# Pooled keys and values in half tiles, their accumulating loads two steps apart, and reciprocals at the end of a step

## The chip, the cores and the metric

The kernel runs on one core of a Trainium2 chip. The metric is the device time of one execution in microseconds (us); lower is better. Three runs of the kernel before gave a median of 1055.34 us (1048.17 to 1058.86). The profile shows one more execution, of 1054.12 us.

## The reference

Attention over keys and values that are averaged in groups of eight, and then a feed-forward layer with a squared relu:

```python
# B, H, S, D = 8, 8, 576, 64; Sp = 72; x: 4608 x 512; w_in: 512 x 2048; w_out: 2048 x 512
k_p = k.reshape(B, H, Sp, 8, D).mean(axis=3)
v_p = v.reshape(B, H, Sp, 8, D).mean(axis=3)
scores = (1 / sqrt(D)) * q @ k_p^T
attn = exp(scores - max(scores)); attn = attn / (sum(attn) + 1e-9)
x = (attn @ v_p), heads side by side
h = maximum(x @ w_in, 0)
out = (h * h) @ w_out
```

## The kernel before, in words

The 4608 tokens are worked through in nine chunks of 512. A chunk has 16 steps, one for each 128 of the 2048 hidden columns (`steps`, L618). In a step PE computes hidden columns (`hidden`, L564, tiles `h`) and then adds the hidden columns of three steps earlier to the outputs (`project`, L596, tiles `o`). From chunk 2 on the hidden product goes by pairs of steps in seven block products (`seven`, L524) on sums and differences of blocks of the input, the operands B11, T1, T2 and so on (`x_operand`, L497, tiles `x_B` and `x_T`). Operands are split in a high and a low part (`split`, L110; `gh` and `gl` for the hidden values), and three products of the parts are added. `w_o`, the weights of the second layer, is kept in DRAM in split form, and each step's 512 KB are fetched over SP's queue, by the program one step before they are used (`fetch_weights`, L208).

Beside it the attention of the next chunk runs, pair of heads by pair of heads, in stages that a table puts on steps (`STEADY`, L83): turning q (`transpose_q`), scores on PE (`sps`), the maximum over keys on POOL (`mx`), exponents, their sum on POOL (`tot`), the sum's way over DRAM into 128 partitions (`rs`, `rc`), the reciprocal on DVE (`reciprocals`, L390, tile `rr`), its way back (`rd`, `rb`), and the product with the values (`weigh_values`, L463, `av`). Within chunk positions 0 to 15, `mx` stands at steps 2, 6, 10, 14, `tot` at 0, 4, 8, 12, the reciprocals at 3, 7, 11, 15.

A batch's pooled keys and values are needed once for each batch. Batches 0 and 1 are loaded at the start; batches 2 to 7 are loaded while other chunks run (`kv_steps`, L724). Eight rows are to be added into one. `load_sums` (L251) does this by four transfers for each kind: the first, on SP's queue, writes two rows of each group side by side; the other three, on POOL's queue, add theirs onto it, each as two transfers of four heads, 144 KB. `pool` (L263) then adds the two on DVE (tiles `kq` and `vp`), and `turn_k` (L273) turns the keys on PE (`kps`). All go through one tile with the tag `two` and one buffer, so the values' first load waits until the keys have been added. By `KV0` and `KV_AT` (L84, L86) the keys' transfers stand at steps 1 to 4 of the chunk two before the one that first needs the batch, their addition at 6 and the turning at 7; the values' transfers at 7 to 10 and their addition at 12.

Every engine works in program order, which the loop at L754 writes out step by step. In a step it emits, in this order: PE's hidden product and attention products; the fetch of `w_o`; the split of hidden values; `project`; the rest of the seven products' sums on DVE; the evacuations of what PE made; the loads (q, `load_sums`); then the other stages in the order of the table, among them `pool` and `reciprocals` (L783); then the relu and square on ACT (`activate`), and last the differences and operands of the next chunk (L795). All plain transfers are issued from SP's queue in that order too, and a transfer that waits holds those behind it. Instructions go through a recording helper, so the profile names L34 for nearly all of them; groups are told apart by tiles.

Of the kernel before, what the change touches and what calls it, by code (L numbers as in the profile page):

```python
# [9 lines left out]
F32 = mybir.dt.float32  # L10
# [4 lines left out]
ALU = mybir.AluOpType  # L15
# [22 lines left out]
def pooled_attn_relu2_ffn(  # L38
# [16 lines left out]
    PE, DVE, ACT, GP, SP = (InOrder(tc, e) for e in (nc.tensor, nc.vector, nc.scalar, nc.gpsimd, nc.sync))  # L55
    B, H, S, D = q.shape
# [4 lines left out]
    POOL = 8  # L61
    SP_ = S // POOL
    NPAIR = H // 2
    NFC = DFF // P
# [16 lines left out]


    STEADY = ((-23, -19, -15, -11), (0, 1, 3, 5, 6, 6, 7, 8))  # L83
    KV0 = -34  # L84
    EARLY = ((-15, -12, -10, -7), (0, 1, 2, 3, 4))
    KV_AT = (("k", 3), ("v", 9))  # L86
    X_AT = (("B11", -9), ("B22", -2), ("T1", -2), ("T3", -2), ("T2", -1), ("B21", -1), ("T4", -1))
    STIR = 10

# [2 lines left out]
    sb = ctx.enter_context(tc.tile_pool(name="sb", bufs=2))  # L92
# [9 lines left out]
    def load(dst, src):  # L102
        loads.append((dst, src))

    def issue_loads():
        for dst, src in loads:
            dma(dst, src)
        loads.clear()
# [67 lines left out]
    def catch_up():  # L176
        while behind:
            behind.pop(0)()
# [36 lines left out]
    def new_batch(b):  # L215
        if b not in kv:
            kv[b] = sb.tile([SP_, H, D], F32, name=f"vp_{b}", tag="vp", bufs=2)
# [28 lines left out]
        for i in range(2):  # L246
            DVE.tensor_reduce(kv[b][:, 2 * p + i, :], t[:, i].rearrange("p (o d) -> p d o", d=D), axis=AX.X, op=ALU.add)

    two = {}

    def load_sums(kind, b, j):  # L251

        if j == 0:
            new_batch(b)
            two[kind] = sb.tile([SP_, H, 2 * D], F32, name=f"{kind}2_{b}", tag="two", bufs=1)
        src = {"k": k, "v": v}[kind][b].rearrange("h (s j o) d -> j s h (o d)", j=POOL // 2, o=2)[j]
        if j == 0:
            load(two[kind], src)
        else:
            for n in range(0, H, H // 2):  # L260
                GP.dma_start(two[kind][:, n:n + H // 2], src[:, n:n + H // 2], accum_op=ALU.add)

    def pool(kind, b):  # L263
        t = two.pop(kind)
        if kind == "v":
            dst = kv[b]
        else:
            dst = sb.tile([SP_, H, D], F32, name=f"kq_{b}", tag="kq", bufs=1)
            for p in range(NPAIR):
                loaded["kp", b, p] = dst[:, 2 * p:2 * p + 2, :]  # L270
        DVE.tensor_tensor(dst, t[:, :, :D], t[:, :, D:], op=ALU.add)

    def turn_k(b, pairs=range(NPAIR)):  # L273

# [26 lines left out]
    def segments(c):  # L301
        t, segs = c * CH, []
        while t < (c + 1) * CH:
            b = t // S
            n = min((b + 1) * S, (c + 1) * CH) - t
            segs.append((b, t - c * CH, n))
            t += n
        return segs
# [255 lines left out]
    def hidden(c, fc):  # L564
        if c < PLAIN:
            hps = [(fc, plain(c, fc))]
        else:
            hps = seven(c, fc)
            if fc % 2 == 0:
                return hps  # L570

        def activate():
            for f, hp in hps:
                if c == 0:
                    r = gts[c, f] = sb.tile([P, CH], F32, name=f"r_{c}_{f}", tag="gl" if f % 2 else "gh", bufs=3)
                else:
                    r = gts[c, f] = sb.tile([P, CH], F32, name=f"r_{c}_{f}", tag="r", bufs=2)
                ACT.activation(r, hp, AF.Relu)
            for f, _ in hps:
                ACT.activation(gts[c, f], gts[c, f], AF.Square)  # L580

        return (activate, None, None) if c >= PLAIN else (None, None, activate)

    def split_hidden(c, fc):
        if c == 0:
            return
        gh = sb.tile([P, CH], F32R, name=f"gh_{c}_{fc}", tag="gh", bufs=3)
        gl = sb.tile([P, CH], F32R, name=f"gl_{c}_{fc}", tag="gl", bufs=3)
        r = gts[c, fc]
        gts[c, fc] = (gh, gl)  # L590
        ACT.copy(gh, r)
        behind.append(lambda: DVE.tensor_tensor(gl, r, gh.bitcast(F32), op=ALU.subtract))
# [3 lines left out]
    def project(c, fc):  # L596
        if fc == 0:
            accs[c] = [ps_o.tile([P, 512], F32, name=f"o_{c}_{t}", tag=f"o{t}") for t in range(NTT)]
        g, key = gts.pop((c, fc)), ("o", fc)
        for t in range(NTT):  # L600
            tt = slice(t * P, (t + 1) * P)
            if c == 0:
                prods = [(g[:, tt], wf[key].rearrange("p a n -> p (a n)"))]
            else:
                prods = [(g[x][:, tt], wt[key][:, w, :]) for x, w in three]
            for i, (a, w) in enumerate(prods):
                PE.matmul(accs[c][t], lhsT=a, rhs=w, start=fc == 0 and i == 0, stop=fc == NFC - 1 and i == len(prods) - 1)

        def store():
            for t in range(NTT):  # L610
                ob = half_tile("ob", f"ob_{c}_{t}")
                ACT.copy(ob, accs[c][t])
                dma(out[c * CH + t * P:c * CH + (t + 1) * P, :], ob)

        return store if fc == NFC - 1 else None
# [5 lines left out]
    def at(step, f, *a):  # L621
        work.setdefault(max(step, -PRO), []).append((f, a))
# [22 lines left out]
    t = ps_a.tile([P, 512], F32, name="stir", tag="a")  # L645
# [60 lines left out]
    t = 1e9  # L706
    for key in reversed(keys):
        t = min(t - 1 / RATE, need[key] - 1 - MARGIN)
# [15 lines left out]
    def kv_steps(b, s):  # L724
        for kind, start in KV_AT:
            for j in range(POOL // 2):
                at(s + start + j, load_sums, kind, b, j)
            at(s + start + POOL // 2 + 1, pool, kind, b)
        at(s + KV_AT[0][1] + POOL // 2 + 2, turn_k, b)

    ready = {0, 1}
    stages = (transpose_q, scores, exponents, send_sums, fetch_sums, reciprocals, fetch_reciprocals, weigh_values)
    for c in range(1, NCH):
        first, offsets = EARLY if c < PLAIN else STEADY
        names = (transpose_q, token_scores, token_normalise, token_turn, weigh_values) if c < PLAIN else stages
        for b, _, _ in segments(c):
            if b not in ready:
                ready.add(b)
                kv_steps(b, c * NFC + KV0)
        if c >= PLAIN:  # L740
            at(c * NFC - 3, x_sums, c)
            for name, d in X_AT:
                at(c * NFC + d, x_operand, c, name)
        for p in range(NPAIR):
            s = c * NFC + first[p]
            at(s - QL, load_q, c, p)
            for d, f in zip(offsets, names):
                at(s + d, f, c, p)


    last = (to_float32, split_quarter, sum_of_quarters, store_weights)
    on_pe = (turn_k, scores, token_scores, token_turn, weigh_values)
    store = None
    for s in range(-PRO, len(steps) + LAG):  # L754
        todo = work.get(s, [])
        soon, then, activate = hidden(*steps[s]) if 0 <= s < len(steps) else (None, None, None)
        later = [f(*a) for f, a in sorted(((f, a) for f, a in todo if f in on_pe), key=lambda x: x[0] is weigh_values)]
        for f, a in todo:
            if f is fetch_weights:
                f(*a)  # L760
        if 0 <= s - 2 < len(steps):
            split_hidden(*steps[s - 2])
        if store:
            store()
        store = project(*steps[s - LAG]) if s >= LAG else None
        if s % 2:
            catch_up()
        if soon:
            soon()
        for f in later:  # L770
            f()
        if then:
            then()
        catch_up()
        first = (load_q, load_sums)
        for f, a in todo:
            if f in (fetch_sums, fetch_reciprocals):
                f(*a)
        for f, a in todo:
            if f in first:  # L780
                f(*a)
        issue_loads()
        for f, a in todo:  # L783
            if f not in first + on_pe + last + (x_sums, x_operand, fetch_weights, fetch_sums, fetch_reciprocals):
                f(*a)
        keys = [a[0] for f, a in todo if f is to_float32]
        if keys:
            to_float32(*keys)
        for f, a in todo:
            if f in last[1:] and f is not sum_of_quarters:  # L790
                f(*a)
        issue_loads()
        if activate:
            activate()
        for kind in (x_sums, x_operand, sum_of_quarters):  # L795
            for f, a in todo:
                if f is kind:
                    f(*a)
# [31 lines left out]
```

## Time and profile before

| what | value |
|---|---|
| median of three runs | 1055.34 us |
| profiled execution, its own time | 1054.12 us |
| span of that execution | 1052.3 us |
| PE busy | 938.6 us, 89% of the span |
| DVE, ACT, POOL busy | 555.3, 509.4, 421.0 us |
| mean granted clock of TensorE | 0.932 |
| time of DMA engines on SP's queue, on POOL's queue | 39.9%, 8.8% of 16 engines' span |

A row of waits reads: engine and tile, what ended the wait, then us in total, times, and the longest. A row of the time line reads: start and duration in us, engine, operation, out<-in, shape, count, and in brackets the engine's idle time just before and what ended it. "issue" means that nothing the profile shows was waited for. A row of windows reads: from and to, length, for each engine busy us and count of instructions, then the mean granted clock (1.00 is full), the DMA engines' share, and GB/s. SPq is SP's queue.

### The profile page before, as it was taken

How to read it: one execution, taken by the hardware profiler on the slowest of the kernel's cores; microseconds unless marked ns; L12 is line 12 of the kernel's file. 1: busy time of each engine (PE TensorE's matmuls, PEld its weight loads, DVE VectorE, ACT ScalarE, POOL GpSimd, SP SyncE). 2: the span in 40 equal slices, each digit the busy share in tenths (PEclk: the TensorE clock that was granted, in tenths of full speed). 3: DMA queues.
4: the chain of work that ended last, by engine and by line, in shares of the span. 5: the costliest groups of instructions: out<-in, count | busy, mean ns of one | idle time of the engine just before them, and what ended most of it. 6: DMA issues, size and time to landing. Idle time of an engine off the chain costs nothing. (4 is left out here: it accounts for less than half of the span.)

```text
span 1052.3 us, 14125 instructions
## 1 busy us (share of the span) xinstructions
PE 938.6 (89%) x5050; PEld 740.4 (70%) x5050; DVE 555.3 (53%) x959; ACT 509.4 (48%) x1015; POOL 421.0 (40%) x234
## 2 busy tenths in 40 slices
PE   5799988995979897988799796979699999999998
PEld 3344443574758676877688685868588888889997
DVE  4884657733567675635274345534375465535231
ACT  2573645553356544644256344544265555535433
POOL 6731124425544455436344554445545333410000
PEclk6598989998989999998899898989899999999999
DMA  8894431484724464465536463546435344223801
GB/s 224 248 255 98 107 99 61 151 223 116 216 56 137 101 158 113 139 124 125 123 113 158 81 151 75 152 93 155 92 121 152 101 134 159 91 93 124 315 1 40
DMA packets 161480, 138.72 MB, mean 132 GB/s; under 512 B 98633, under 2 KB 126281, under 8 KB 161409
## 3 DMA queue, kind: packets, MB, share of 16 engines
q1 hardware_dynamic: 132608, 127.13, 39.9%
q0 software_dynamic: 28800, 10.68, 8.8%
q8 instruction: 40, 0.66, 0.2%
q14 instruction: 32, 0.25, 0.1%
HBM read 119.65 MB, written 18.06 MB: 131 GB/s over the span
## 5 line engine op out<-in xcount | busy, mean ns | idle before, releaser
L34 PE MATMUL o<-w_o,gh 128*128 128x512 f32 x1024 | 330.0, 404 | 8.2 <-DMA w_o<-kept 8.1
L34 POOL PARTITION_ALL_REDUCE tot<-sc x56 | 191.9, 3474 | 178.0 <-issue 153.4
L34 PEld LDWEIGHTS o<-w_o,gh 128*128 128x128 f32 x1024 | 189.6, 194 | 54.8 <-issue 13.3
L34 PE MATMUL o<-w_o,gl 128*128 128x512 f32 x512 | 203.4, 397 | 0.0
L34 PE MATMUL h<-x_T,w_S 128*128 128x256 f32 x1008 | 136.7, 290 | 3.3 <-DVE x_T L34 1.7
L34 ACT ACTIVATE r<-h 128x512 f32<-128x512 f32 x144 | 85.1, 594 | 110.9 <-PE h L34 57.2
L34 POOL PARTITION_ALL_REDUCE mx<-sc x56 | 108.4, 1982 | 64.4 <-ACT sc L34 63.2
L34 PEld LDWEIGHTS h<-x_T,w_S 128*128 128x128 f32 x1008 | 130.2, 199 | 5.3 <-DVE x_T L34 2.9
L34 PE MATMUL h<-x_B,w_A 128*128 128x256 f32 x672 | 101.7, 288 | 31.1 <-ACT r L34 31.1
L34 DVE TENSOR_TENSOR gl<-r,gh 128x512 fp32r<-128x512 f32 x128 | 108.1, 858 | 34.6 <-ACT gh L34 34.6
L34 PEld LDWEIGHTS h<-x_B,w_A 128*128 128x128 f32 x672 | 94.0, 196 | 37.2 <-ACT r L34 33.2
L34 PEld LDWEIGHTS o<-w_o,gl 128*128 128x128 f32 x512 | 98.6, 193 | 22.3
L34 ACT COPY u<-h 128x256 f32<-128x256 f32 x112 | 41.6, 371 | 134.0 <-DVE h L34 79.2
L34 DVE TENSOR_TENSOR h<-h,u 128x256 f32<-128x256 f32 x168 | 72.7, 433 | 51.2 <-ACT u L34 29.4
L34 POOL DMA_DIRECT2D k<-in_k_dram x36 | 43.7, 1214 | 125.2 <-issue 119.3
L34 POOL DMA_DIRECT2D v<-in_v_dram x36 | 44.2, 1227 | 120.1 <-issue 62.9
L34 ACT ACTIVATE sc<-sc 72x512 f32<-72x512 f32 x56 | 34.5, 631 | 117.8 <-DVE sc L34 117.8
L34 ACT ACTIVATE r<-r 128x512 f32<-128x512 f32 x144 | 84.2, 625 | 1.0
L34 ACT CAST gh<-r 128x512 fp32r<-128x512 f32 x128 | 78.6, 614 | 1.0 <-PE o L34 0.4
L34 DVE TENSOR_TENSOR u<-h,u 128x256 f32<-128x256 f32 x56 | 23.7, 423 | 80.5 <-ACT u L34 79.6
L34 PE MATMUL o<-wf_o,r 128*128 128x512 f32 x128 | 65.1, 656 | 0.0
L34 DVE TENSOR_TENSOR st<-qs,st 64x512 fp32r<-64x512 f32 x56 | 46.9, 837 | 25.1 <-ACT st L34 24.3
(89 smaller groups left out, 1204.1 us busy)
## 6 DMA issues: line engine op xcount, KB each, us to landing
w_o<-kept SPq DMA_DIRECT2D x128, 512.0 KB
out_dram<-ob SPq DMA_DIRECT2D x36, 256.0 KB
raw_i<-in_moe_w_in_dram SPq DMA_DIRECT2D x16, 512.0 KB
raw_o<-in_moe_w_out_dram SPq DMA_DIRECT2D x16, 512.0 KB
kept<-w_o SPq DMA_DIRECT2D x16, 512.0 KB
rb<-rd SPq DMA_DIRECT2D x56, 128.0 KB
k<-in_k_dram POOLq DMA_DIRECT2D x36, 144.0 KB, 4.1
v<-in_v_dram POOLq DMA_DIRECT2D x36, 144.0 KB, 5.4
```

What stands on the lines that cost most here:

```text
L34: return lambda *a, **k: self.tc.keep_in_program_order(f(*a, **k))
```

## The change

Three things change. The tile `two` becomes two tiles of four heads with two buffers, in the same space as before; the first load is split in two as well, and `pool` adds in two halves, each from its own tile. The accumulating transfers stand two steps apart: the keys' at steps 15 (of the chunk before), 1, 3 and 5, their addition at 7 and the turning at 8; the values' at 7, 9, 11 and 13, their addition at 15. And `reciprocals` leave the middle of the step for its end, behind the operands of the next chunk, with the transfer `rd` that they issue.

```diff
     STEADY = ((-23, -19, -15, -11), (0, 1, 3, 5, 6, 6, 7, 8))
-    KV0 = -34
     EARLY = ((-15, -12, -10, -7), (0, 1, 2, 3, 4))
-    KV_AT = (("k", 3), ("v", 9))
+    KV_AT = (("k", -33), ("v", -25))
...
-    two = {}
+    two, HALF = {}, H // 2
 
     def load_sums(kind, b, j):
 
         if j == 0:
             new_batch(b)
-            two[kind] = sb.tile([SP_, H, 2 * D], F32, name=f"{kind}2_{b}", tag="two", bufs=1)
         src = {"k": k, "v": v}[kind][b].rearrange("h (s j o) d -> j s h (o d)", j=POOL // 2, o=2)[j]
-        if j == 0:
-            load(two[kind], src)
-        else:
-            for n in range(0, H, H // 2):
-                GP.dma_start(two[kind][:, n:n + H // 2], src[:, n:n + H // 2], accum_op=ALU.add)
+        for n in range(2):
+            if j == 0:
+                two[kind, n] = sb.tile([SP_, HALF, 2 * D], F32, name=f"{kind}2_{b}_{n}", tag="two", bufs=2)
+                load(two[kind, n], src[:, n * HALF:(n + 1) * HALF])
+            else:
+                GP.dma_start(two[kind, n], src[:, n * HALF:(n + 1) * HALF], accum_op=ALU.add)
 
     def pool(kind, b):
-        t = two.pop(kind)
...
-        DVE.tensor_tensor(dst, t[:, :, :D], t[:, :, D:], op=ALU.add)
+        for n in range(2):
+            t = two.pop((kind, n))
+            DVE.tensor_tensor(dst[:, n * HALF:(n + 1) * HALF], t[:, :, :D], t[:, :, D:], op=ALU.add)
...
             for j in range(POOL // 2):
-                at(s + start + j, load_sums, kind, b, j)
-            at(s + start + POOL // 2 + 1, pool, kind, b)
-        at(s + KV_AT[0][1] + POOL // 2 + 2, turn_k, b)
+                at(s + start + 2 * j, load_sums, kind, b, j)
+            at(s + start + POOL, pool, kind, b)
+        at(s + KV_AT[0][1] + POOL + 1, turn_k, b)
...
-                kv_steps(b, c * NFC + KV0)
+                kv_steps(b, c * NFC)
...
-            if f not in first + on_pe + last + (x_sums, x_operand, fetch_weights, fetch_sums, fetch_reciprocals):
+            if f not in first + on_pe + last + (x_sums, x_operand, reciprocals, fetch_weights, fetch_sums, fetch_reciprocals):
                 f(*a)
...
-        for kind in (x_sums, x_operand, sum_of_quarters):
+        for kind in (x_sums, x_operand, reciprocals, sum_of_quarters):
```

POOL, the keys of batch 5, before (steps 2 to 6 of chunk 3; ISA rows are all-reduces, `mx` the maximum and `tot` the sum of a pair of heads, DMA rows the accumulating transfers):

```order
L34 ISA mx_2_0_3503<-sc_2_3502 72x512
L34 ISA mx_2_1_3504<-sc_2_3502 72x512
L34 DMA k_5_3434<-in_k_dram 72x4x128 x6
L34 ISA tot_2_0_3650<-sc_2_3502 72x512
L34 ISA tot_2_1_3651<-sc_2_3502 72x512
L34 ISA mx_3_0_3771<-sc_3_3770 72x512
L34 ISA mx_3_1_3772<-sc_3_3770 72x512
```

The same after the change, from step 0 on:

```order
L34 ISA tot_1_0_3401<-sc_1_3246 72x512
L34 ISA tot_1_1_3402<-sc_1_3246 72x512
L34 DMA k_5_0_3314<-in_k_dram 72x4x128
L34 DMA k_5_1_3315<-in_k_dram 72x4x128
L34 ISA mx_2_0_3525<-sc_2_3524 72x512
L34 ISA mx_2_1_3526<-sc_2_3524 72x512
L34 DMA k_5_0_3314<-in_k_dram 72x4x128
L34 DMA k_5_1_3315<-in_k_dram 72x4x128
L34 ISA tot_2_0_3668<-sc_2_3524 72x512
L34 ISA tot_2_1_3669<-sc_2_3524 72x512
L34 DMA k_5_0_3314<-in_k_dram 72x4x128
L34 DMA k_5_1_3315<-in_k_dram 72x4x128
```

The six transfers in one run have become three pairs, the first ahead of `mx_2` and the last behind `tot_2`.

POOL, the values of the same batch, before (from step 8 of chunk 3):

```order
L34 DMA v_5_3844<-in_v_dram 72x4x128 x2
L34 ISA tot_3_0_3922<-sc_3_3770 72x512
L34 ISA tot_3_1_3923<-sc_3_3770 72x512
L34 DMA v_5_3844<-in_v_dram 72x4x128 x2
L34 ISA mx_0_0_4046<-sc_0_4045 72x512
L34 ISA mx_0_1_4047<-sc_0_4045 72x512
L34 DMA v_5_3844<-in_v_dram 72x4x128 x2
```

And after the change:

```order
L34 ISA tot_3_0_3943<-sc_3_3790 72x512
L34 ISA tot_3_1_3944<-sc_3_3790 72x512
L34 DMA v_5_0_3847<-in_v_dram 72x4x128
L34 DMA v_5_1_3848<-in_v_dram 72x4x128
L34 ISA mx_0_0_4067<-sc_0_4066 72x512
L34 ISA mx_0_1_4068<-sc_0_4066 72x512
L34 DMA v_5_0_3847<-in_v_dram 72x4x128
L34 DMA v_5_1_3848<-in_v_dram 72x4x128
L34 ISA tot_0_0_4196<-sc_0_4066 72x512
L34 ISA tot_0_1_4197<-sc_0_4066 72x512
L34 DMA v_5_0_3847<-in_v_dram 72x4x128
L34 DMA v_5_1_3848<-in_v_dram 72x4x128
```

The three pairs each stand one all-reduce later; the last one now stands behind `tot_0`.

DVE, the end of chunk 5 (from step 15's `gl`; `rr` is the reciprocal, the xf row with two sources the difference that becomes T2, then the low parts of T2, B21 and T4), before:

```order
L34 TENSOR_TENSOR gl_13_6477<-r_13_6361,gh_13_6476 128x512
L34 TENSOR_SCALAR rr_0_6509<-rc_0_6498 128x8
L34 RECIPROCAL rr_0_6509<-rr_0_6509 128x8
L34 TENSOR_TENSOR xf_1_6082<-xf_1_6082,xf_0_5538 128x2x256
L34 TENSOR_TENSOR x_T_6515<-xf_1_6082,x_T_6515 128x512
L34 TENSOR_TENSOR x_B_6518<-xf_1_6082,x_B_6518 128x512
L34 TENSOR_TENSOR xf_1_6082<-xf_1_6082 128x2x256
L34 TENSOR_TENSOR x_T_6522<-xf_1_6082,x_T_6522 128x512
```

And after the change:

```order
L34 TENSOR_TENSOR gl_13_6511<-r_13_6393,gh_13_6510 128x512
L34 TENSOR_TENSOR vp_5461<-v_7_0_5995 72x256
L34 TENSOR_TENSOR vp_5461<-v_7_1_5996 72x256
L34 TENSOR_TENSOR xf_1_6115<-xf_1_6115,xf_0_5573 128x2x256
L34 TENSOR_TENSOR x_T_6546<-xf_1_6115,x_T_6546 128x512
L34 TENSOR_TENSOR x_B_6549<-xf_1_6115,x_B_6549 128x512
L34 TENSOR_TENSOR xf_1_6115<-xf_1_6115 128x2x256
L34 TENSOR_TENSOR x_T_6553<-xf_1_6115,x_T_6553 128x512
L34 TENSOR_SCALAR rr_0_6556<-rc_0_6532 128x8
L34 RECIPROCAL rr_0_6556<-rr_0_6556 128x8
```

The values' addition, in two halves, stands where the reciprocal stood, ahead of T2; before it stood in step 12. The reciprocal has gone behind T4.

## Prediction

> **What bounds the kernel now.** I read first what PE waited for, then DVE's waits, then the time line around PE's longest gaps, and last a stretch without gaps. Steps are numbered within a chunk, 0 to 15.
>
> ```profile
> PE h L34 <- ACT r L34: 35.8, 6, 8.6
> PE kps L34 <- DVE kq L34: 27.3, 5, 6.9
> ...
> PE o L34 <- DMA w_o<-kept: 8.1, 8, 3.8
> PE sps L34 <- DVE st L34: 7.4, 5, 3.8
> DVE rr L34 <- DMA rc<-rs: 65.0, 16, 6.7
> DVE vp L34 <- DMA v<-in_v_dram: 50.8, 5, 11.4
> DVE kq L34 <- DMA k<-in_k_dram: 40.4, 6, 10.2
> ```
>
> PE's gaps are few and long: 35.8 us before hidden products, in six waits, and 27.3 us before the turning of the keys, in five. DVE waits for transfers at two additions, vp and kq, about once a batch each. How these belong together is seen on the last batch:
>
> ```profile
> 747.76 1.21 POOL L34 DMA_DIRECT2D v<-in_v_dram  x1 [4.74 <-issue]
> 753.30 0.69 DVE L34 TENSOR_TENSOR vp<-v 72x512 f32<-72x512 f32 x1 [11.37 <-DMA v<-in_v_dram]
> 756.91 0.58 PE L34 MATMUL h<-x_B,w_A 128*128 128x256 f32 x1 [8.52 <-ACT r L34]
> ```
>
> DVE stands 11.37 us at step 12's addition of the values. Behind it in DVE's order are a subtraction for the exponents and gl, which frees the tile that ACT writes r into; ACT can't empty PSUM, and PE stands 8.52 us at step 14.
>
> ```profile
> 676.83 1.26 POOL L34 DMA_DIRECT2D k<-in_k_dram  x1
> ...
> 701.93 1.20 POOL L34 DMA_DIRECT2D k<-in_k_dram  x1 [2.89 <-issue]
> 702.68 7.58 POOL L34 PARTITION_ALL_REDUCE tot<-sc  x2
> 706.71 0.71 PE L34 MATMUL kps<-ident,kq 72*128 72x72 f32 x4 [5.83 <-DVE kq L34]
> ```
>
> The six accumulating transfers of the keys leave POOL one behind the other, 25.1 us over five spacings, 5.0 each. Even the second half of a pair waits, though it writes other bytes. The sum queued behind them, tot, starts at 702.68, when PE is already standing.
>
> What a batch costs, and what a stretch without gaps looks like:
>
> ```profile
> 590.70:706.70 116.00, 99.18 (x596) 86.03 (x597) 55.90 (x98) 52.56 (x103) 55.70 (x29) 0.93 0.52 121
> 772.80:865.20 92.40, 92.40 (x578) 80.71 (x579) 53.65 (x90) 50.35 (x98) 41.24 (x16) 1.00 0.40 123
> 176.30:179.30 3.00, 2.98 (x10) 0.50 0.18 72
> ...
> 756.90:763.00 6.10, 6.09 (x28) 0.50 0.00 1
> sum 50.60, PE 50.53; mean PE 4.21
> ```
>
> Sixteen steps with a batch's loads took 116.0 us, sixteen without 92.4. The last three rows are from twelve windows, one behind each of PE's twelve gaps over 3 us from 172 us on: PE works there at a granted clock of 0.50 (0.62 in one), 50.5 us in all, so some 25 us are lost beside the gaps.
>
> **What could come back.** The two kinds of gaps, 35.8 + 27.3; the waits for w_o and sps, 8.1 + 7.4, most of them right behind a late key or value; less 3 for short ones elsewhere: 76. With the clock's 25 it is 101 us, if every such wait went.
>
> **The change part by part.** *The transfers themselves.* From issue to landing, k first, then v:
>
> ```profile
> DMA to landing us min/median/max: 3.7/4.1/9.7
> DMA to landing us min/median/max: 3.8/5.4/8.6
> ```
>
> Part of k's low median is from transfers beside a standing PE, so I take the 5.0 from start to start for k, and 5.7 for v: its median and 0.3 until the next starts. I keep the halves of a pair one behind the other, since the trace shows that wherever two stand together.
>
> The Trainium skill, "DMA: Bandwidth & Descriptors", section "Anatomy of one DMA — SWDGE (gpsimd) path", gives 2.0 us and the bytes over 436 GB/s for such a transfer, by estimate 2.3 us for 144 KB. The trace has about twice that; by the page the sum would be the first rival's, 958.
>
> *Keys.* The pairs now stand at steps 1, 3 and 5, the addition at 7, the turning at 8. I lay them into the stretch without gaps:
>
> ```profile
> 779.82 6.45 POOL L34 PARTITION_ALL_REDUCE tot<-sc  x2 [12.29 <-issue]
> ...
> 802.23 6.45 POOL L34 PARTITION_ALL_REDUCE tot<-sc  x2 [10.21 <-issue]
> ...
> 825.60 6.45 POOL L34 PARTITION_ALL_REDUCE tot<-sc  x2 [10.20 <-issue]
> 834.76 3.96 POOL L34 PARTITION_ALL_REDUCE mx<-sc  x2 [2.72 <-ACT sc L34]
> 848.78 6.45 POOL L34 PARTITION_ALL_REDUCE tot<-sc  x2 [10.05 <-issue]
> 821.62 0.63 PE L34 MATMUL o<-w_o,gh 128*128 128x512 f32 x2
> ```
>
> POOL ends step 0's tot at 786.3. First pair at 786.3 and 791.3; 0.75 later POOL is free (701.93 to 702.68 above); mx, 3.96, to 796.0; second pair at 796.3 and 801.3; step 4's tot starts on time, at 802.2, and takes up to 7.6 beside a transfer, to 809.8; third pair at 809.8 and 814.8, landed at 819.5, added by 819.9. DVE stands meanwhile, with only an operand of the next chunk, a reciprocal and the next step's sums behind it. PE wants kq before step 8's o, at 821.6. Spare: 1.7, so the keys' gap costs 0. The bounds: 4.4 from start to start ends 2 us earlier and gives nothing more; 6.3 ends at 826.2 and costs 4.5.
>
> *Values.* The pairs stand at steps 9, 11 and 13, the addition at 15. POOL ends step 8's tot at 832.05: pair at 832.05 and 837.75; mx from 838.5 to 842.5; second pair at 843.5, behind the first's landing, and 849.2; tot at 849.9, 1.1 late, to 857.5; third pair at 857.5 and 863.2, landed at 868.6. What is queued behind the addition is new:
>
> ```profile
> 863.33 0.64 DVE L34 TENSOR_TENSOR xf<-xf,xf 128x512 f32<-128x512 f32 x1
> 865.36 0.69 DVE L34 TENSOR_TENSOR x_T<-xf,x_T 128x512 fp32r<-128x512 f32 x1 [1.39 <-ACT x_T L34]
> 865.83 1.38 PE L34 MATMUL h<-x_T,w_S 128*128 128x256 f32 x8
> ```
>
> The addition stands just before the xf of 863.33, the difference that becomes operand T2, and PE multiplies T2 from about 866: no slack today. With the values landed at 868.6, half an addition (0.35), xf (0.64), ACT's copy (0.6) and x_T (0.69) end at 870.9: PE stands 4.9 us at the chunk's start, where it stood about 8.5 at step 14 before. So the stall is not taken away but made smaller, and put elsewhere. It counts for four batches. The batch loaded in chunk 1 has longer steps round it (twelve products of 128x512 each), and the first one belongs to a chunk that needs no T2: 0 for both. Four times 4.9 is 20, and four times 2 of half clock is 8 (from the 25 us behind twelve gaps). The bounds: at 4.4 from start to start the third pair lands at 863.7 and costs nothing; at 6.3 it lands at 871.6 and costs 8.
>
> The first batch's addition moves from step 12 to 15, behind the last product that reads the old buffer; that wait is gone, and with it the 3.8 of sps, the longest in its row above.
>
> *Reciprocals.* They leave the middle of the step for its end. DVE's 65.0 us of waits for rc lie mostly at steps 3 and 11, where nothing is put ahead of them: not gained. At step 15 they now come behind T2, B21 and T4, some 5.5 us later, and SP's queue holds rd, and behind it the fetch of w_o, as long:
>
> ```profile
> 718.02 0.37 SPq L34 DMA_DIRECT2D w_o<-kept  x1
> 721.89 0.50 PE L34 MATMUL o<-w_o,gh 128*128 128x512 f32 x1 [0.81 <-DMA w_o<-kept]
> 863.83 0.43 SPq L34 DMA_DIRECT2D w_o<-kept  x1
> 874.25 0.72 PE L34 MATMUL o<-w_o,gh 128*128 128x512 f32 x2
> ```
>
> The fetch of 863.83 would go at 869.4. One took 3.9 from issue to use (718.02 to 721.89): there at 873.3, needed at 874.25. At step 7 the values' first load now waits on SP for the later kq, with rd and a w_o behind it, also about in time. I put 5 us for both places together, over seven and five chunks; 0 and 15 are the bounds.
>
> *Small things.* Twelve more issues on SP, 0.37 each, and the additions in halves of half the length: hidden beside PE; 5 us if SP had no slack at all.
>
> **Sum.** 101 − 20 − 8 − 5 = 68. The profiled execution took 1054.1 us by its own time, 1.8 more than its span, and is 1.2 below the median of the three runs: 1054 − 68 = **986 us**.
>
> **The rivals.**
> *Transfers are shorter, or halves go together.* With tiles of their own and no wait in the program, the two halves could be in flight at once, or each takes k's median. The last values then land before 864, nothing stands at the chunk's start: 28 us less, 958. For it: 4.1 and the 3.7 and 3.8 of the fastest. Against: before, too, no semaphore held the second half.
> *The wait comes back.* Transfers beside a PE that never stands take 6 us, since fetches of w_o and q then come denser; POOL's pairs and all-reduces push one another on. Then 32 + 10 for the values, 18 + 8 for the keys, 5 for SP: 28 gained, 1026. For it: v's 5.4 where PE runs. Against: 5.0 over the keys' spacings.
> *Slower.* The reciprocals at the end of their step hold SP's queue so long that each time the next w_o is late. There are 28. It decides when each costs PE more than 68/28 = 2.4 us; at 3.8, the longest such wait seen, it is 986 + 106 = 1092. Against: only at steps 7 and 15 does anything stand ahead of them.
> *The change doesn't do what it says.* POOL runs in order, so the transfers could stay bunched. The order above refutes it: one or two all-reduces stand between pairs.
>
> **How the numbers follow.** The forecast has 0.53, with a range of its own from 968 to 1008; the first rival 0.22, the wait that comes back 0.19, slower 0.03, and 0.03 for no change by some mixture. The range 955 to 1028 leaves some 0.15 out. A change of 1% is about what three runs can tell here. Faster by more: 0.92; within: 0.04; slower: 0.04.
>
> **What would show it.** PE's wait for kq gone or under 5 us in all; its waits for ACT's r gone, and a new one at h from DVE's x_T at the starts of chunks 3 to 6, 3 to 6 us each; DVE's waits for k and v below half; the pairs on POOL still with a gap inside each; the clock at 1.00 between chunk starts. It is wrong if PE waits longest for w_o, if kq still holds PE, or if the halves start together.

## The result, and the profile after

The changed kernel took 966.64 us, the median of four runs (961.6 to 974.69), beside 1056.41 us for the kernel before (four runs, 1048.17 to 1058.86): a ratio of 0.917, 95% interval 0.909 to 0.925. The profiled execution took 968.37 us by its own time, with a span of 966.6 us, 85.7 less than the span before. The prediction was a gain of 68 us. The time lies in its range of 955 to 1028, 19 us under the predicted 986 and 1.4 under the range of 968 to 1008 that the forecast had for itself.

First, what PE and DVE waited for after the change (engine, tile, what ended the wait; us in total, times, longest):

```profile
PE h L34 <- ACT x_T L34: 11.6, 5, 4.1
...
PE o L34 <- DMA w_o<-kept: 2.7, 5, 0.8
...
PE h L34 <- ACT r L34: 1.2, 1, 1.2
...
DVE kq L34 <- DMA k<-in_k_dram: 16.6, 7, 4.2
DVE vp L34 <- DMA v<-in_v_dram: 9.2, 3, 4.4
```

The row of kps for DVE's kq (27.3 before) is gone, h for ACT's r has fallen from 35.8 to one wait of 1.2, and a row that was 1.3 before has grown: h for ACT's x_T, 11.6 in five. DVE's waits for keys and values fell from 40.4 and 50.8 to 16.6 and 9.2.

The page's busy time, and three stretches: a chunk with a batch's loads, one without, and one of the places behind a gap:

```profile
PE 917.7 (95%) x5050; PEld 729.4 (75%) x5050; DVE 568.1 (59%) x971; ACT 511.1 (53%) x1015; POOL 413.2 (43%) x234
```

```profile
502.60:604.30 101.70, 97.16 (x599) 85.11 (x598) 57.36 (x99) 53.08 (x103) 54.28 (x28) 0.97 0.57 138
797.80:886.60 88.80, 88.80 (x547) 77.76 (x546) 40.15 (x75) 42.12 (x84) 18.44 (x7) 1.00 0.37 119
...
484.00:487.40 3.40, 3.40 (x17) 3.30 (x16) 2.37 (x6) 1.41 (x3) 0.00 (x0) 0.50 0.02 1
```

Sixteen steps with loads now take 101.7 us where they took 116.0. The second stretch has less attention beside it (18 us of POOL's work) than the prediction's 92.4 us (41); from 691.2 to 783.6, with as much attention, PE does 580 products in 92.4 us, where it did 578. Of the 85.7 us, PE's busy time gives 20.9 (938.6 to 917.7: the same products at a clock that is less often at half), and its idle time the other 64.8 (113.7 to 48.9).

How the values now leave POOL, on the last batch (the time line; start and duration, and in brackets the idle time before):

```profile
648.43 1.25 POOL L34 DMA_DIRECT2D v<-in_v_dram  x1
652.82 1.22 POOL L34 DMA_DIRECT2D v<-in_v_dram  x1 [3.14 <-DVE gl L34]
...
658.44 1.24 POOL L34 DMA_DIRECT2D v<-in_v_dram  x1 [0.87 <-issue]
665.09 1.22 POOL L34 DMA_DIRECT2D v<-in_v_dram  x1 [5.41 <-ACT gh L34]
...
672.76 1.24 POOL L34 DMA_DIRECT2D v<-in_v_dram  x1
678.57 1.21 POOL L34 DMA_DIRECT2D v<-in_v_dram  x1 [4.57 <-DVE gl L34]
679.33 3.98 POOL L34 PARTITION_ALL_REDUCE mx<-sc  x2
```

Between the pairs, where lines are left out, stand mx and tot, as the prediction laid them out, and inside each pair there is still a gap. The spacings are 4.4, 6.7 and 5.8 us; 5.7 was taken for all.

The stall that is left, at the start of chunk 5, on DVE and on PE:

```profile
581.39 0.42 DVE L34 TENSOR_TENSOR vp<-v 72x256 f32<-72x256 f32 x1 [4.38 <-DMA v<-in_v_dram]
581.73 0.68 DVE L34 TENSOR_TENSOR xf<-xf,xf 128x512 f32<-128x512 f32 x1
583.10 0.69 DVE L34 TENSOR_TENSOR x_T<-xf,x_T 128x512 fp32r<-128x512 f32 x1 [0.69 <-ACT x_T L34]
```

```profile
583.12 4.72 PE L34 MATMUL h<-x_T,w_S 128*128 128x256 f32 x18 [4.07 <-ACT x_T L34]
```

This is the predicted place and chain: the second half of the values lands late, the addition waits, the difference xf and operand T2 stand behind it, and PE has nothing to multiply. It is the longest of the five; the others, in order of time, are 0.88 (chunk 2), 2.05, 1.86 and 2.76 us (chunks 3, 4 and 6). DVE waited for the values at three of the five places, 1.01, 4.38 and 3.85 us ahead of chunks 4, 5 and 6. Ahead of chunks 2 and 3 it didn't; there DVE itself was late. For chunk 3:

```profile
378.16 3.17 DVE L34 TENSOR_TENSOR x_T<-xf,x_T 128x512 fp32r<-128x512 f32 x2
381.86 1.59 DVE L34 TENSOR_TENSOR vp<-v 72x256 f32<-72x256 f32 x2
```

Two x_T take 3.17 us here and 1.29 ahead of chunks 4 to 6, and the two halves of the addition 1.59, where they take 0.75 ahead of chunk 2; what they stood beside is told with the run that moves the addition behind the operands.

### The profile page after: what moved, and what is told of

The parts are those of the page before. It is cut to its first block, busy times and chain, and to the rows that moved or that the text cites. A ratio compares the mean times of both kernels' runs of the same rounds, so it can differ in the third digit from the quotient of the medians.

```text
span 966.6 us, 14156 instructions
## 1 busy us (share of the span) xinstructions
PE 917.7 (95%) x5050; PEld 729.4 (75%) x5050; DVE 568.1 (59%) x971; ACT 511.1 (53%) x1015; POOL 413.2 (43%) x234
## 4 chain that ended last, share of the span: by engine, by line
PE 59%; DVE 10%; issue 9%; POOL 7%; DMA 7%; ACT 6%; SPq 2%; DVEq 0%; POOLq 0%; ACTq 0%
PE o L34 28%; PE h L34 25%; POOL tot L34 4%; PE av L34 3%; PE sps L34 3%; DMA w_o<-kept 3%; SPq L34 2%; POOL mx L34 1%; DVE gl L34 1%; ACT sc L34 1%; DMA v<-in_v_dram 1%; DMA rc<-rs 1%; POOL k L34 1%; POOL v L34 1%; DVE h L34 1%
## 5 line engine op out<-in xcount | busy, mean ns | idle before, releaser
L34 PE MATMUL o<-w_o,gh 128*128 128x512 f32 x1024 | 324.3, 398 | 2.7 <-DMA w_o<-kept 2.7
L34 POOL PARTITION_ALL_REDUCE tot<-sc x56 | 184.6, 3344 | 175.9 <-issue 157.7
L34 PEld LDWEIGHTS o<-w_o,gh 128*128 128x128 f32 x1024 | 186.2, 190 | 47.4 <-issue 7.3
L34 PE MATMUL o<-w_o,gl 128*128 128x512 f32 x512 | 200.6, 392 | 0.0
L34 PE MATMUL h<-x_T,w_S 128*128 128x256 f32 x1008 | 137.9, 292 | 13.4 <-ACT x_T L34 11.6
L34 DVE TENSOR_TENSOR gl<-r,gh 128x512 fp32r<-128x512 f32 x128 | 122.6, 973 | 35.5 <-ACT gh L34 35.5
L34 POOL PARTITION_ALL_REDUCE mx<-sc x56 | 111.3, 2035 | 41.0 <-ACT sc L34 40.2
L34 PE MATMUL h<-x_B,w_A 128*128 128x256 f32 x672 | 98.5, 283 | 1.2 <-ACT r L34 1.2
L34 PEld LDWEIGHTS h<-x_B,w_A 128*128 128x128 f32 x672 | 92.0, 191 | 5.9 <-ACT r L34 1.6
L34 PE MATMUL o<-wf_o,r 128*128 128x512 f32 x128 | 62.5, 634 | 0.0
L34 PE MATMUL h<-x,wf_i 128*128 128x512 f32 x128 | 58.9, 604 | 0.1
```

Source lines behind the costliest of these rows:

```text
L34: return lambda *a, **k: self.tc.keep_in_program_order(f(*a, **k))
```

## The experiments

All ratios are against runs of the kernel before on the same chip, with 95% intervals. Four kernels take the change apart.

### Half tiles alone

The steps and the reciprocals as before, only `load_sums` and `pool` with tiles of four heads:

```diff
-            two[kind] = sb.tile([SP_, H, 2 * D], F32, name=f"{kind}2_{b}", tag="two", bufs=1)
...
+                two[kind, n] = sb.tile([SP_, HALF, 2 * D], F32, name=f"{kind}2_{b}_{n}", tag="two", bufs=2)
```

> The kernel before with the half tiles alone: two tiles with two buffers, same steps, reciprocals where they were. My theory: the transfers on POOL still follow each other, about 5 us from start to start, since no semaphore held the second half before either; the waits at kq and vp stay, 1050 to 1062 us. Rival: tiles of their own let the halves fly together; then the keys' six transfers take about 15 us in place of 25 and most of PE's 27 us before kps goes: under 1025 us.

Measured: 1041.24 us, ratio 0.988 (0.985 to 0.992), a gain of some 13 us. Neither expectation had that.

```profile
PE kps L34 <- DVE kq L34: 25.3, 9, 4.0
PE h L34 <- ACT r L34: 23.1, 7, 8.3
PE o L34 <- DMA w_o<-kept: 13.3, 8, 4.4
```

The halves did not go together, and kps hardly gained: its five waits became nine short ones, since the pairs of heads of the first half are turned while the second is on its way. What fell is h for r (35.8 to 23.1), and w_o gave part back. In the last batch of before, 5.5 us lie between the issue of the values' first load and POOL's first transfer behind it; here, with half as many bytes, 4.5. The rest of the shorter stall at the values couldn't be put down to one cause, and it stays open.

### New steps alone

Whole tiles, reciprocals in their old place, only the new table and spacing:

```diff
-    KV0 = -34
-    KV_AT = (("k", 3), ("v", 9))
+    KV_AT = (("k", -33), ("v", -25))
...
-                at(s + start + j, load_sums, kind, b, j)
-            at(s + start + POOL // 2 + 1, pool, kind, b)
+                at(s + start + 2 * j, load_sums, kind, b, j)
+            at(s + start + POOL, pool, kind, b)
...
```

> The kernel before with the new steps alone (transfers two steps apart, additions at steps 7 and 15), one whole tile, reciprocals where they were. My theory: the steps carry nearly all of the gain: 965 to 985 us, PE's wait for kq gone. Rival: the whole tile with one buffer holds the first load of the values until all of the keys are added and the gain needs the half tiles: over 1000 us.

Measured: 967.86 us, ratio 0.918 (0.914 to 0.922). The steps alone give all of the change's gain. The 13 us of the half tiles are not added on top; what they shorten in the old steps is a stall that the new steps take away. With whole tiles PE's waits do lie elsewhere:

```profile
PE o L34 <- DMA w_o<-kept: 9.7, 7, 3.6
PE h L34 <- ACT x_T L34: 5.1, 5, 2.4
```

That is 7.0 us more for w_o and 6.5 less at the chunk starts than in the changed kernel, at the same time.

### Reciprocals at the end alone, and the change without that

The first is the kernel before with only the two tuples of the loop changed; the second the changed kernel with these two lines as before.

```diff
-        for kind in (x_sums, x_operand, sum_of_quarters):
+        for kind in (x_sums, x_operand, reciprocals, sum_of_quarters):
```

> The kernel before with the reciprocals at the end of their step alone. My theory: no change that can be told, 1047 to 1062 us, because DVE's waits for rc lie where nothing is put ahead of them. Rival one: freeing DVE from 65 us of waits for rc gives 15 us or more, under 1040 us. Rival two: the later rd holds SP's queue and w_o comes late, over 1065 us.

> The changed kernel with the reciprocals back in the middle of their step. My theory: within 5 us of the changed kernel, 962 to 977 us; at step 15 the reciprocal stands again ahead of operand T2, so PE's wait for x_T grows by up to 0.5 us at each chunk start. Rival: waits for rc ahead of T2 cost 3 us or more at each chunk start, over 980 us.

Measured: 1049.93 us, ratio 0.998 (0.994 to 1.002), for the first; 968.03 us, 0.920 (0.915 to 0.924), for the second. Where the reciprocals stand makes no difference that can be measured, in either kernel. The rival in which they hold SP's queue is refuted.

### Keys alone, values alone

The changed kernel, but only one of the two kinds gets two steps between its transfers; the other has its old steps. For the keys alone (for the values alone the same the other way round, with the keys' start at -31 and the turning a step after their addition):

```diff
+            n = 2 if kind == "k" else 1
             for j in range(POOL // 2):
-                at(s + start + 2 * j, load_sums, kind, b, j)
-            at(s + start + POOL, pool, kind, b)
+                at(s + start + n * j, load_sums, kind, b, j)
+            at(s + start + (POOL if n == 2 else 5), pool, kind, b)
```

> The changed kernel with the new steps for the keys alone; the values' transfers stand at steps 7 to 10 and their addition at 12 as before. Theory (the two stalls are separate, and each is worth its gaps and the half clock behind them): PE's wait for kq is gone, the wait of h for ACT's r at step 14 stays at about 30 us; gain some 35 to 45 us, 1009 to 1019. Rival (POOL's queue joins them: with the keys spread out the values start no earlier, but the sums before them are on time): values nearly on time too, under 1000.

> The changed kernel with the new steps for the values alone; the keys' transfers stand at steps 1 to 4, their addition at 6 and the turning at 7 as before. Theory (separate stalls): PE's wait for kps stays, about 20 to 27 us with the half clock behind it, the wait for ACT's r goes, some 10 us at the chunk starts come; gain 40 to 50 us, 1004 to 1014. With the run of the keys alone the two gains add up to that of both, some 87 us. Rival: the keys' stall alone also sets the values' (they wait for the tile): gains add up to far less than 87.

Measured: keys alone 983.92 us, ratio 0.935 (0.931 to 0.940); values alone 1001.97 us, 0.952 (0.947 to 0.957). Beside 1054.53 us that is 70.6 and 52.6 us, together 123, where both give 86 to 90 in the runs above. The gains do not add up to that of both, nor to far less, as the rival of the values' run had it, but to more. Some of that is the half tiles, which both kernels have. Against the half tiles alone (0.988) the ratios give 56, 39 and, for both, 75 us: 95 against 75, so some 20 us come with either change. The rival of the keys' run holds, by which one stall feeds the other. What waits with the keys alone:

```profile
PE o L34 <- DMA w_o<-kept: 10.2, 6, 3.4
PE sps L34 <- DVE st L34: 9.7, 7, 3.8
...
PE h L34 <- ACT r L34: 7.4, 9, 2.9
...
DVE vp L34 <- PE av L34: 32.6, 6, 12.2
DVE vp L34 <- DMA v<-in_v_dram: 3.8, 3, 2.4
```

The values' transfers and their addition at step 12 are the old ones, and yet DVE waits 3.8 us for them instead of 50.8, and PE 7.4 for r instead of 35.8 (23.1 with the half tiles alone). At step 12 the addition now waits for PE's product `av` instead, which still reads the old buffer: 12.2 and 7.7 us in the first two batches, 3.0 to 3.3 in each of the others, where before it stood 7.2 to 11.4 for the values. So most of what the half tiles leave of the values' stall came from the keys: six transfers in a row end late, the sum and the maximum queued behind them on POOL run late, and the values' first pair starts behind those. In the last batch the values' last half left POOL at 676.03, 0.7 us behind step 12's first product of T2 (675.36); before, at 747.76, it was 10.6 us behind it (737.21). With the values alone the keys' row stays, as expected, and the chunk starts have their 9.8:

```profile
PE kps L34 <- DVE kq L34: 28.2, 10, 3.9
PE h L34 <- ACT x_T L34: 9.8, 5, 3.5
```

### Late additions, but transfers in a row

The additions at steps 7 and 15 and the turning at 8, as in the changed kernel, with the transfers one step apart as before:

```diff
-    KV_AT = (("k", -33), ("v", -25))
+    KV_AT = (("k", -31), ("v", -25))
...
-                at(s + start + 2 * j, load_sums, kind, b, j)
-            at(s + start + POOL, pool, kind, b)
-        at(s + KV_AT[0][1] + POOL + 1, turn_k, b)
+                at(s + start + j, load_sums, kind, b, j)
+            at(s + start + (6 if kind == "k" else 8), pool, kind, b)
+        at(s + KV_AT[0][1] + 7, turn_k, b)
```

> The changed kernel with half tiles and late additions (steps 7 and 15, turning at 8), but the transfers one step apart as in the kernel before: keys at steps 1 to 4, values at 7 to 10. Tells what the gain comes from: the later due time of the addition, or the free slots between transfers on POOL. Theory A (the due time alone counts; keys' last pair landed about 10 us after the old turning was due, values' about as late, and the new ones come two and three steps later): keys land before step 8's turning or a few us late, values land well before step 15, so the chunk starts have no stall; 950 to 975. Theory B (the spread counts: six transfers in a row hold the sums queued behind them on POOL for about 25 us, exponents and weights come late, and PE waits for those): over 985, with PE's waits at sps, av or at h for ACT's r.

Measured: 1006.05 us, ratio 0.957 (0.952 to 0.962). The later due time, with the half tiles that this kernel has too, is worth 48 us (half tiles alone gave 13), and some 40 more need the spread. Theory B had the time, but not the place of the wait, which is w_o, 40.9 us in ten. Five of the ten, one a batch, are of 6.5 to 7.7 us. One of these, on POOL, on SP's queue and on PE:

```profile
424.72 1.25 POOL L34 DMA_DIRECT2D k<-in_k_dram  x1
...
450.38 1.19 POOL L34 DMA_DIRECT2D k<-in_k_dram  x1 [3.07 <-ACT r L34]
451.13 7.24 POOL L34 PARTITION_ALL_REDUCE tot<-sc  x2
```

```profile
454.81 3.83 SPq L34 DMA_DIRECT2D rs<-tot  x2
458.69 0.35 SPq L34 DMA_DIRECT2D w_o<-kept  x1
```

```profile
462.03 1.22 PE L34 MATMUL o<-w_o,gh 128*128 128x512 f32 x2 [6.95 <-DMA w_o<-kept]
```

The six transfers hold POOL from 424.7 to 451.1; step 4's sum, tot, ends at 458.4; its way to DRAM, rs, waits for it at the head of SP's queue, and the fetch of w_o stands behind rs. PE waits 6.95 us for a fetch that left as soon as rs had gone. In the kernel before tot stood behind the keys in the same way (702.68 in the prediction's lines), but PE was then standing for kps already.

### The addition behind the operands

The changed kernel, with the values' addition moved from ahead of T2 to just ahead of the reciprocals at the end of step 15 (`pool_v` calls `pool("v", b)`):

```diff
-        for kind in (x_sums, x_operand, reciprocals, sum_of_quarters):
+        for kind in (x_sums, x_operand, pool_v, reciprocals, sum_of_quarters):
```

> The changed kernel, but the addition of the values stands behind the operands T2, B21 and T4 of the next chunk at the end of step 15, just ahead of the reciprocals. Theory (what is left of the old stall is the values' addition standing ahead of T2, once a batch): the waits of h for ACT's x_T at the chunk starts, 11.6 us, and the half clock behind them, some 8 us lost, go; about 950 us, 944 to 957, and no wait of PE at a chunk start over 1 us. Rival (T2 is late by itself, since DVE and ACT are full at step 15; or the keys' next first load on SP, which waits for this addition, now holds the fetch of w_o behind it): the waits stay or move to w_o, 962 to 975.

Measured: 964.07 us, ratio 0.916 (0.911 to 0.922): no gain that can be told from the change itself. The theory's 950 was wrong.

```profile
PE h L34 <- ACT x_T L34: 5.6, 4, 1.9
...
PE o L34 <- DMA w_o<-kept: 4.6, 5, 2.3
```

The stall at the chunk starts fell by 6.0 us, so the place of the addition was half of it, and w_o took 1.9 back. What made T2 late with nothing of the values ahead of it, on DVE and on POOL:

```profile
479.58 3.20 DVE L34 TENSOR_TENSOR x_T<-xf,x_T 128x512 fp32r<-128x512 f32 x2
...
483.31 1.52 DVE L34 TENSOR_TENSOR xf<-xf,xf 128x512 f32<-128x512 f32 x1
```

```profile
480.00 1.21 POOL L34 DMA_DIRECT2D v<-in_v_dram  x1 [4.34 <-DVE x_B L34]
480.76 4.27 POOL L34 PARTITION_ALL_REDUCE mx<-sc  x2
```

Two x_T take 3.20 us where two alone take 1.29, and an xf 1.52 instead of 0.69, while POOL's two maxima run. That belongs to the change: the same operand, over all 28 of its instructions (ns, shortest/median/longest), first before and then after:

```profile
L34 DVE TENSOR_TENSOR x_T<-xf,x_T x28: 676/688/693, 308.9 to 958.6; 128x512 fp32r<-128x512 f32 x28
```

```profile
L34 DVE TENSOR_TENSOR x_T<-xf,x_T x28: 679/692/2571, 277.7 to 872.6; 128x512 fp32r<-128x512 f32 x28
```

Step 14's maximum stands behind the values' third pair on POOL, and so it starts in the moment in which DVE makes the operands.

The Trainium skill, "SBUF — State Buffer", section "SBUF: two separate sides", says that DVE and GpSimd share one pair of ports, which one of them holds for a whole instruction while the other is blocked, and that a DVE instruction with two inputs from SBUF is such a case. The trace agrees with it in part: 2571 ns beside an all-reduce, 693 at most before. But at 682.55 the addition takes its 0.42 us inside the last batch's maximum, which runs from 679.33 to 683.31:

```profile
682.55 0.42 DVE L34 TENSOR_TENSOR vp<-v 72x256 f32<-72x256 f32 x1 [3.85 <-DMA v<-in_v_dram]
```

That it is this pair of ports and nothing else, no run here shows.

### T2 multiplied last, alone and with the addition behind

In a chunk's first pair of hidden products only:

```diff
-            product(b, "S2", "T2")
+            if fc:
+                product(b, "S2", "T2")
             product(u, "S3", "T3", True)
             product(d, "S1", "T1")
+            if not fc:
+                product(b, "S2", "T2")
```

> The changed kernel, but in the first pair of hidden products of a chunk PE multiplies operand T2 last of the four instead of second, some 2.8 us later; the addition of the values stays ahead of T2. Theory (the stalls at chunk starts, 11.6 us in all, come from T2's being late, by the values' addition and by DVE's work stretching beside POOL's all-reduce of step 14): stalls of 0.88, 2.05, 1.86, 4.07 and 2.76 us shrink by up to 2.8 each, to about 1.3 in all, and most of the half clock behind them goes; 950 to 957. Rival (T3 or T1 are then late in its place, or the sums of that pair on DVE): no gain, 963 to 972.

> The changed kernel with both: the addition of the values behind the operands, and T2 multiplied last of the four in a chunk's first pair. After the addition had been put behind, 5.6 us of waits for ACT's x_T were left, at most 1.9 each, with DVE's x_T and xf at 1.5 to 2.7 us where alone they take 0.68, beside POOL's mx. Theory: with 2.8 us of room these go too; no wait at a chunk start, the time 945 to 955. Rival (what moves behind the addition, the reciprocals and w_o's fetch, becomes the bound): w_o's waits of 4.6 us stay or grow, and the time is 958 to 968.

Measured: alone 962.57 us, ratio 0.912 (0.910 to 0.915); with the addition behind as well 963.65 us, 0.914 (0.911 to 0.916). In the first, PE waited for

```profile
PE o L34 <- DMA w_o<-kept: 5.4, 5, 2.4
PE h L34 <- DVE h L34: 3.7, 5, 0.8
```

The row for ACT's x_T, the stall at the chunk starts, has fallen to 0.5 in the first and is gone in the second. The mean granted clock tells little: 0.964 to 0.971 over the runs of the first and 0.964 to 0.989 over those of the second, where the changed kernel had 0.956 to 0.968. About a third of the stall comes back as waits for DVE's sums of that pair, 0.7 to 0.8 each, and, in the second, up to 2.0 (8.1 in six), about as much as the addition's move could have given. The ratio of T2 last alone is 0.005 under the change's own, some 5 us, and lies within that one's interval: a gain that is likely, smaller than expected, and not settled.

### Transfers of half the size

The changed kernel, with each accumulating transfer of four heads cut in two of two heads:

```diff
-                GP.dma_start(two[kind, n], src[:, n * HALF:(n + 1) * HALF], accum_op=ALU.add)
+                for m in range(0, HALF, HALF // 2):
+                    GP.dma_start(two[kind, n][:, m:m + HALF // 2], src[:, n * HALF + m:n * HALF + m + HALF // 2], accum_op=ALU.add)
```

> The changed kernel with each accumulating transfer of four heads cut in two of two heads, 72 KB each, four to a step. Tests why a second transfer leaves POOL only behind the landing of the first though no semaphore holds it. Theory (POOL's queue has room for the pieces of one such transfer, not of two: 288 pieces of 512 bytes each): two transfers of half the size fit together, so the second leaves about 1.3 us after the first, before that has landed, and the third waits; four take as long as two did, 8 to 10 us, and the time stays at 960 to 972. Rival (accumulating transfers follow one another whatever their size): each leaves some 0.3 us behind the landing of the one before, four to a step take 12 us or more by a fixed share of 3 us each, POOL's sums and the additions come late, and the time is over 980.

Measured: 971.24 us, ratio 0.920 (0.918 to 0.923).

```profile
400.39 2.35 POOL L34 DMA_DIRECT2D k<-in_k_dram  x2
405.01 2.31 POOL L34 DMA_DIRECT2D k<-in_k_dram  x2 [2.26 <-issue]
```

```profile
DMA to landing us min/median/max: 3.0/4.4/9.4
```

Two transfers of 72 KB are issued back to back, 2.35 us for both, and the fastest of all took 3.0 from issue to landing: the second leaves before the first has landed. The third waits. With 144 KB each transfer stood alone. So the wait inside a pair is not one of the accumulation but of size: POOL's queue takes 144 KB at once, two transfers of 72, and not 216 or 288. Two quarters take as long as one half did (4.6 us from pair to pair here), so nothing is won.

### Transfers of q ahead of the values' first load

On top of T2 multiplied last, the order of SP's queue in step 7:

```diff
-        for f, a in todo:
-            if f in first:
-                f(*a)
+        for kind in first:
+            for f, a in todo:
+                if f is kind:
+                    f(*a)
```

> The kernel with T2 multiplied last in a chunk's first pair, and now step 7's eight transfers of q stand on SP's queue ahead of the values' first loads, which wait there for the keys' addition. Theory (the last waits for w_o, 5.4 us in five, come from this queue: the values' load waited until 625.3, eight issues of q took 0.46 each behind it, then rd, and the fetch of w_o left at 630.2, for a product that stood until 634.2): the fetch leaves 3 to 4 us earlier, PE's waits for w_o fall below 2 us, with the half clock behind the longest; 948 to 956 in the profile, and a median some 4 us under that of T2 last alone. Rival (w_o waits for its buffer or its own transfer, or q's transfers now run beside the keys' last pair and make it later): no change, 957 to 966.

Measured: 960.92 us, ratio 0.910 (0.906 to 0.915), the lowest of all.

```profile
PE o L34 <- DMA w_o<-kept: 1.3, 2, 0.7
```

The waits for w_o fell from 5.4 to 1.3 us: the cause was the place in the queue. Other rows took as much back: sps for DVE's st rose from 3.5 to 5.1, h for ACT's x_T from 0.5 to 1.7, kps for kq from 0.6 to 1.6. The time moved by less than the intervals hold (0.912 to 0.910) and lies where the rival had it, so the row is shown and the gain is not.

## Why the prediction was right, and where its sizes were off

The direction, the places and the mechanism held. Of the gain of 85.7 us in the spans, 17.7 were not foreseen, and the prediction's own terms tell where they lie.

**What could come back.** The rows did: h for r fell by 34.6 us, kps by 27.3, w_o by 5.4, sps by 3.6. Of sps 7.4 had been counted. The clock gave 20.9 net of what is still lost, where 25 − 8 = 17 was the sum: 3.9 more. The 8 were right: behind the four longer stalls PE worked 17.0 us at a granted clock of 0.50 (3.4, 3.4, 6.8 and 3.4), which loses some 8, and between chunk starts, from 389 to 482 and from 488 to 582 us, the clock was 1.00 as foreseen.

**The keys' gap costs 0.** Right. DVE still stands up to 4.2 us for the keys at step 7, and PE doesn't notice.

**The values' stall moves to the chunk starts.** The chain was named instruction by instruction and was seen so at chunks 4 to 6; moving either end of it (the addition, or the product of T2) made it shrink or go. Its size is the step that failed: four times 4.9, 20 us, against a growth of the row by 10.3. This is 9.7 of the 17.7 us. Counted from the end of step 8's tot, the sum let the last half leave POOL after 31.2 us and land after 36.6. On the last batch (tot from 642.11 for 6.45) it left after 30.0, at 678.57, and DVE went on after 34.0, at 682.55. So the larger error is the landing of that half: 4.0 us, and 4.0 to 4.5 over the four batches, where the median of all transfers, 5.4, was taken. The rest is the first pair, 4.2 to 4.4 from start to start instead of 5.7, of which the second pair, 5.8 to 6.9, took a part back. The chain also has a second cause that the sum lacks, DVE's work beside POOL's maximum. At chunks 4 to 6 it cost nothing, since DVE then stood for the landing all the same. At chunk 2, whose batch was put at 0, two instructions took 2.1 us more beside the maximum, which is enough for the 0.88. At chunk 3 the last half landed at 382.60, while DVE was still at the addition's first half; by these times, an estimate, it added some 0.4 to the 2.05. Of the signs, 3 to 6 us at each of chunks 3 to 6 was seen at chunk 5 alone, and the operand's part that PE waited for was ACT's, not DVE's.

**SP's queue and w_o.** 8.1 less 5 was 3.1; the row fell by 5.4, 2.3 more. The bound of 15 was never near, and the last run above shows where such waits come from, in the kernel with T2 last: the first load of the values, waiting for the keys' addition, with w_o behind it.

**Reciprocals: no gain.** Right, in both kernels.

**Half tiles.** They were given nothing of their own. In the old steps that was wrong by 13 us; in the new ones, right.

**The rest**, 1.8 us, is a balance. The sps row gave 3.8 less than was counted and h for r 1.2 less; but the rows had been taken at 76 where they add up to 78.6, and small rows gave 4.2, such as kps for ACT's te, 1.8 before and gone after.

**What the sum did not need, and the reader does.** The prediction treated keys and values as two stalls with a price each, 27.3 and 35.8. For both together the sum came out; for the keys alone it would have been some 30 us short (35 to 45 in the expectation above, 70.6 measured). Of these 30 the half tiles may be 13; the rest is there because much of the values' stall was the keys' lateness handed on by POOL's queue.

**The rivals.** The measured 966.64 is nearer to the first rival's 958 than to the 986. Its mechanism was not seen: no two halves of 144 KB went together, in any kernel, and from issue to landing the medians were 5.2 us (keys) and 5.3 (values), not k's old 4.1. But the last halves of the values did take 4.0 to 4.5, so in the one transfer that sets the stall it was half right. The wait that comes back fell short: 5.6 to 6.9 us from start to start, near its 6, were there in the values' second and third pairs, but only 4.2 to 4.4 in the first, and PE stood 11.6 us for them, not the rival's 32. The slower one is refuted by the two runs with the reciprocals moved alone.

## What to carry to other kernels

When two long waits follow each other on one in-order queue, price them together: taking the first away may take most of the second with it, and the sum of their rows is not what each is worth. A transfer or all-reduce that is moved within such a queue is to be judged by what stands behind it, on its own engine and on the queues that wait for that; here 25 us of transfers in a row made a weight fetch late that had no tie to them. After a due time has been moved, look for the next thing that stands behind the waiting instruction, as T2 did here, and see whether its use, not its making, can be put later.

## What the runs showed of the hardware

Room in POOL's queue. An accumulating transfer of 144 KB (72 rows by four heads, 512 bytes each) was never joined by a second before it had landed, in any kernel; the next left 0.3 us later at the earliest. Two of 72 KB were in flight together, and the third waited.

DVE beside POOL's all-reduce. Operands of two inputs, 0.69 us alone, took up to 2.57 us. It isn't every one: in the changed kernel from 300 us on, of 25 such instructions (x_T, x_B, xf, gl, and the scores' subtraction) beside a maximum, 3 took longer, 1.5 to 2.6 us, and none of the three began more than 0.4 us behind it; of 22 beside a sum, 20 did, 1.8 to 3.7. With POOL idle none of 150 took over 0.69.

The clock. A gap of 1.86 us, with one of 0.34 close behind it, was enough for 3.4 us at half rate:

```profile
482.67 0.38 PE L34 MATMUL h<-x_T,w_S 128*128 128x256 f32 x1 [1.86 <-ACT x_T L34]
```

In the window from 484.0 above the granted clock is 0.50 though PE works through all of it. A gap of 0.88 us in an earlier chunk, also with 0.34 behind it, left no such trace. The Trainium skill, "TensorE: Matmul & The Clock Gate", section "Part 1: The HAM clock gate (the "warmup" mystery)", has the rate fall after an idle window of about 3.4 us; the length of the slow stretch agrees with that window, the idle time that it took does not, and here the measurement decides.
